# Probability tiles as places for weight pieces, and another order in the first three steps of an attention and soft mixture-of-experts kernel

## The chip, the cores and the metric

The kernel runs on 1 core of one Trainium2 chip, in one launch. The metric is device time in microseconds (us); lower is better. Engines: TensorE (PE, with its weight loads as PEld), VectorE (DVE), ScalarE (ACT), GpSimd (POOL) and SyncE (SP), which here issues all transfers but one. The trace's line numbers are those of the kernel before.

## The reference

First block-sparse attention over 4 batches, 8 heads, 768 positions of width 64. Each query sees the keys less than 16 positions away, and 24 summaries: for each block of 32 keys the elementwise maximum, and for the values the mean. Then a soft mixture of experts over the 3072 rows of width 512.

```python
k_sum = k.reshape(B, H, nb, block, D).max(axis=3)
v_sum = v.reshape(B, H, nb, block, D).mean(axis=3)
scores_l = where(|i - j| < 16, scale * q @ k.T, -1e9)
scores_s = scale * q @ k_sum.T + log(block)
a = softmax(concat(scores_l, scores_s));  x = a @ concat(v, v_sum)

logits = x @ phi                              # 3072 rows, 32 slots
slot_input = softmax(logits, axis=0).T @ x    # 8 experts, 4 slots each
slot_out[e] = relu(slot_input[e] @ w1[e]) @ w2[e]
out = softmax(logits, axis=1) @ slot_out
```

## The kernel before, in words

**Layout.** A head block is half a batch: four heads. There are 8 of them, each in 3 steps of 256 queries (two tiles of 128), so 24 steps. For each chunk of 64 queries, one product covers the chunk's own 64 keys and 64 further columns: edge keys (16 to either side) and the 24 block keys. Own keys, edges and block keys lie in one tile per head block, `kk`, of which there are two; edges and block keys stand there once for each of the six query tiles of a head block. `k_max` (L177) takes the block maxima on VectorE in six parts, `k_put` (L201) copies them into the place of each query tile, `k_edge` (L189) copies the edges. The sums of the values (`v_sum`, "V" in the plan) are products on TensorE, a ScalarE copy and VectorE additions; `put_v` (L343) copies them into each step's value tile on GpSimd.

**A step** (the loop at L526). For step i: scores on TensorE (L230); the scan (L249), in which VectorE adds the mask and takes the maximum, 8 tiles; the exponential on ScalarE, for half of the tiles after a subtraction on GpSimd (`soft_sub`, L265). Then step i-1's probabilities are transposed on TensorE (`trans`, L271) and copied by ScalarE (`evac`, L276), and step i-2's products with the values follow (`values`, L287), with their normalisation on VectorE (`norm`, L308). PLAN (L41) says in which step the parts that belong to the experts' routing ("X", "L", "T", "D") and the value sums ("V") are put, before or after the values. Each engine runs its instructions in the order in which this loop writes them; a wait holds what is queued behind it on that engine. Each step's scores reuse the same two banks, so the scores of step i+1 wait for the scan of step i.

**Transfers.** SyncE issues keys, queries, values and weights, in the order in which the code writes them, each after a wait for its place. A step's value tile is one of seven and is loaded anew seven steps later.

**Weights.** w1 and w2 make 64 pieces of 512 KB. `room` (L128) lists the places for them: 20 tiles of their own, and tiles of the attention that are done, each with the step from which it may be taken; NPRE is their count. Piece k goes to place k modulo NPRE (`load_piece`, L137). LOADS (L63) says how many are issued in each step, and `loads(...)` (L589, L596, L614, L626) those behind the loop. The first product (L661) takes 32 pieces and after each issues the next load; the second (L699) takes the other 32, interleaved by END with the products that make the output (L725). The output leaves in ten transfers of 512 KB and, for the last two blocks of rows, four of 256 KB.

**Start.** A few products on zeros (L502) run while the first keys arrive. Then the maxima, edges (GpSimd) and block keys (VectorE) of head block 0, then the steps.

Of the kernel before, what the change touches and what calls it, by code (L numbers as in the profile page):

```python
# [9 lines left out]
F32 = mybir.dt.float32  # L10
# [8 lines left out]
NB = S // 32  # L19
HB = 2 * B  # L20
TPS = 3
NSTEP = HB * TPS
NTT = 2 * TPS
# [15 lines left out]


PLAN = {  # L41
    0: "| V0",
    2: "| V1",
    5: "| V2",
    6: "X0 X1 |",
# [14 lines left out]
}  # L60


LOADS = [0, 0, 0, 0, 1, 1, 1, 1, 1, 1, 1, 1, 1, 1, 1, 1, 1, 1, 1, 3, 3, 3, 3, 5]  # L63

# [8 lines left out]
def attention_soft_moe(  # L75
# [12 lines left out]
    nc = tc.nc  # L88
    NQ = NT // 512

    const = ctx.enter_context(tc.tile_pool(name="const", bufs=1))
    att = ctx.enter_context(ExitStack())
    wk = att.enter_context(tc.tile_pool(name="wk", bufs=2, side="right"))
# [21 lines left out]
    qs = [qb[:, n] for n in range(NQR)]  # L115
    vs = [const.tile([128, 2, 2, 4, 65], F32, name=f"v{n}") for n in range(NV)]
    xs = [const.tile([128, 2, 512], F32, name=f"x{n}") for n in range(NX)]
    was = [const.tile([128, 1024], F32, name=f"wa{n}") for n in range(NWA)]


    pieces = [("w1", e, c) for e in range(NE) for c in range(4)] + [("w2", n) for n in range(32)]
    vflat = [v.rearrange("p c t h d -> p (c t h d)")[:, 0:1024] for v in vs]
    qall = qb.rearrange("p n t r k -> p (n t r k)")
    qflat = [qall[:, 1024 * n : 1024 * n + 1024] for n in range(3)]
    xflat = [x.rearrange("p t c -> p (t c)") for x in xs]
    kflat = [[k[:, 1024 * n : 1024 * n + 1024] for n in range(3)] for k in kk]

    room = [(t, 0) for t in was] + [(vflat[3], 19), (vflat[4], 20)] + [(t, 20) for t in kflat[0] + [qflat[0]]]  # L128
    room += [(vflat[5], 21), (xflat[2], 21), (vflat[6], 22), (vflat[0], 23)]
    room += [(t, 23) for t in kflat[1] + qflat[1:]] + [(vflat[1], 24), (vflat[2], 25)]  # L130
    room += [(t, 26) for t in xflat[3:]] + [(t, 27) for t in xflat[0:2]]
    NPRE = len(room)
    slots_ = [t for t, _ in room]
# [23 lines left out]
    def load_q(hb, part=slice(0, TPS)):  # L157
        if hb < HB:
            nc.sync.dma_start(out=qs[hb % NQR][:, part], in_=qx[hb, :, part])
# [11 lines left out]
    def eview(hb, c):  # L171
        e0 = (EA0, 0)[c]
        return kk[hb % 2][:, e0 : e0 + NEH].rearrange("p (r t k) -> p r t k", r=2, t=NTT)

    kst = {}

    def k_max(hb, part):  # L177
        if hb >= HB:
            return
        if hb not in kst:  # L180
            kst[hb] = wk.tile([128, 2, NB], F32, name="ks", bufs=2)
        pr, th = part // 3, part % 3
        nc.vector.reduce_max(  # L183
            out=kst[hb][:, pr, 8 * th : 8 * th + 8],
            in_=kview(hb)[:, pr, 16 + 256 * th : 272 + 256 * th].rearrange("p (b k) -> p b k", k=32),
            axis=AX,
        )

    def k_edge(hb, eng):  # L189
        if hb >= HB:  # L190
            return
        k = kview(hb)
        for c in range(2):
            e = eview(hb, c)[:, :, :, 32 * c : 32 * c + 32]
            for half in range(2):
                o = 64 * c + 80 * half
                src = k[:, :, o : o + 128 * (NTT - 1) + 16]
                src = bass.AP(src.tensor, src.offset, [src.ap[0], src.ap[1], [128, NTT], [1, 16]])
                eng.tensor_copy(out=e[:, :, :, 16 * half : 16 * half + 16], in_=src)  # L199

    def k_put(hb, eng):  # L201
        if hb >= HB:
            return
        for c in range(2):
            o = 0 if c else 32
            eng.tensor_copy(  # L206
                out=eview(hb, c)[:, :, :, o : o + NB], in_=kst[hb].unsqueeze(2).broadcast_to([128, 2, NTT, NB])
            )

    def keys(hb, r, c, pr, t):  # L210
# [29 lines left out]
    def soft_max(i, r):  # L240
        hb, tp = steps[i]
        s = ps_[i][r]
        m = wk.tile([128, 4], F32, name="m", bufs=4)
        p = wk.tile([128, 4, 128], F32, name="p", bufs=4)
        for u in range(4):
            t = 2 * tp + u // 2
            mk = 0 if t == 0 else 2 if t == NTT - 1 else 1

            nc.vector.tensor_tensor_reduce(  # L249
                out=p[:, u, :], in0=s[:, u, :], in1=maskv[:, mk, :], scale=-0.125, scalar=-NEG,  # L250
                op0=ALU.add, op1=ALU.min, accum_out=m[:, u : u + 1],
            )
        p_[i, r] = p, m
# [18 lines left out]
        ptr_[i, r] = pt  # L272

    def evac(i, r, eng=None):
        ptr = wk.tile([128, 4, 128], F32, name="ptr", bufs=4)
        (eng or nc.scalar.copy)(out=ptr, in_=ptr_[i, r])  # L276
        ptr_[i, r] = ptr

# [64 lines left out]
    def put_v(i, c, eng):  # L343
        n0 = 0 if c else 96
        src = vsst[0:NB, i // TPS % 2].rearrange("n h c -> n (h c)").unsqueeze(1)
        eng.tensor_copy(  # L346
            out=vs[i % NV][n0 : n0 + NB, c].rearrange("n t h c -> n t (h c)"), in_=src.broadcast_to([NB, 2, 260])
        )
# [136 lines left out]
    def flush(gs):  # L485
        for g in gs:
            while advance(g):
                pass
# [3 lines left out]
    def begin(names):  # L492
        gs = [pieces_of[n[0]](int(n[1:])) for n in names.split()]
        for g in gs:
            advance(g)
        return gs
# [7 lines left out]
    load_k(0, 1)  # L504
    load_q(0, slice(0, 1))
    nc.scalar.dma_start(out=cs, in_=cst)
    for i in range(TPS):
        load_v(i)
    load_q(0, slice(1, TPS))
    load_k(1, 0)  # L510
    load_k(1, 1)
    for hb in range(2):
# [5 lines left out]
    for part in range(6):  # L518
        k_max(0, part)
    k_edge(0, nc.gpsimd)  # L520
    k_put(0, nc.vector)
    nc.gpsimd.memset(W1ST, 0.0)


# [1 line left out]
    for i in range(NSTEP):  # L526
        a, b = i - 1, i - 2
        front, back = (PLAN.get(i, "|")).split("|")
        hb, tp = i // TPS, i % TPS
        now[0] = i  # L530
        scores(i)
        if i < TPS:
            load_q(1, slice(tp, tp + 1))
            for n in ((3, 4), (5,), (6,))[i]:
                load_v(n)
        load_q(hb + 2, slice(tp, tp + 1))
        if tp == 2:
            load_k(hb + 2, 0)
        if tp == 0 and hb > 0:
            load_k(hb + 1, 1)  # L540
        held = [g for g in held if advance(g)]
        soft_max(i, 0)
        soft_exp(i, 0)
        flush(held)
        if a >= 0:
            for c in range(2):
                put_v(a, c, nc.gpsimd)
        for n in range(LOADS[i]):
            if now[0] < 19:
                load_piece(True)  # L550
        if tp == 2:
            k_put(hb + 1, nc.gpsimd)
        soft_max(i, 1)
        if i < NSTEP - 1:
            soft_sub(i, 1)
        if tp == 1:
            k_edge(hb + 1, nc.gpsimd)
        if a >= 0:
            trans(a, 0)
            trans(a, 1)  # L560
            evac(a, 0)
            evac(a, 1, nc.vector.tensor_copy if i == NSTEP - 1 else None)
        flush(begin(front))
        soft_exp(i, 1)
        if b >= 0:
            values(b)
            norm(b)
        if tp < 2:
            for part in ((0, 1, 2), (3, 4, 5))[tp]:
                k_max(hb + 1, part)  # L570
        held = begin(back)
        if b >= 0:
            load_v(b + NV)
        for _ in range(LOADS[i]):
            if now[0] >= 19:
                load_piece()


    def loads(step, n):
        now[0] = step  # L580
        for _ in range(n):
            load_piece()
# [3 lines left out]
        put_v(j, c, nc.gpsimd)  # L586
    trans(j, 0)
    values(j - 1)
    loads(24, 4)  # L589
    evac(j, 0)  # L590
    trans(j, 1)
    evac(j, 1)
    gx = begin("X18 X19")
    norm(j - 1)
    values(j)
    loads(25, 1)  # L596
    flush(gx)
    tail.append(1)
    norm(j)
# [30 lines left out]
    fin = ctx.enter_context(tc.tile_pool(name="fin", bufs=2, side="right"))  # L630
# [8 lines left out]

    for q0, n in ((0, 4), (4, 2)):  # L640
        l = lt[:, q0 : q0 + n].rearrange("p q t -> p (q t)")
        ct = fin.tile([128, 512], F32, name="ct")[:, 0 : 128 * n]
        cv = ct.rearrange("p (b s) -> p b s", s=NE * 4)
        cm = fin.tile([128, 16], F32, name="cm")[:, 0 : 4 * n]
        cz = fin.tile([128, 16], F32, name="cz")[:, 0 : 4 * n]
        nc.vector.transpose(out=ct, in_=l)
        nc.vector.reduce_max(out=cm, in_=cv, axis=AX)
        nc.vector.tensor_tensor(out=cv, in0=cv, in1=cm.unsqueeze(2).broadcast_to([128, 4 * n, 32]), op=ALU.subtract)
        nc.scalar.activation(out=ct, in_=ct, func=AF.Exp)
        nc.vector.reduce_sum(out=cz, in_=cv, axis=AX)  # L650
        nc.vector.tensor_scalar_add(out=cz, in0=cz, scalar1=EPS)
        nc.vector.reciprocal(out=cz, in_=cz)
        nc.vector.tensor_tensor(out=cv, in0=cv, in1=cz.unsqueeze(2).broadcast_to([128, 4 * n, 32]), op=ALU.mult)
        nc.vector.transpose(out=l, in_=ct)

    hps = pf.tile([128, 512], F32, name="hps", tag="pf")[:, 0:256]
    for k in range(32):
        _, e, c = pieces[k]
        t = wt[k].rearrange("p (j f) -> p j f", j=4)
# [177 lines left out]
```

## Time and profile before

| | |
|---|---|
| median of 3 runs | 194.75 us (194.31 to 195.47) |
| the profiled execution | 194.69 us, of which span 192.9 us |
| TensorE busy | 168.3 us (87%) |
| VectorE, ScalarE, GpSimd busy | 121.0, 94.5, 72.1 us |
| moved by DMA | 66.36 MB, mean 344 GB/s |
| mean granted TensorE clock | 0.957 |

The span runs from the first to the last instruction. Busy times overlap, as the engines work side by side. A granted clock of 1.0 is TensorE's full speed, 0.5 half of it. A DMA share near 1 means that all 16 DMA engines have a packet under way nearly all the time.

### The profile page before, as it was taken

To read this page: it belongs to the slowest core of one execution; us is meant where nothing else is said; L and a number is where in the kernel's file an instruction comes from. 1 tells how busy PE (TensorE), PEld (TensorE's weight loads), DVE (VectorE), ACT (ScalarE), POOL (GpSimd) and SP (SyncE) were. 2 spreads that over 40 slices of the span, in tenths; PEclk is the share of its full clock that TensorE was granted. 3 is DMA by queue.
4 is the path that set the end of the run, shared out by engine and by line. 5 is a ranking of instruction groups with operands and counts; after the bars stand their busy time and mean duration, and the time that the engine had idled before them with its cause. 6 is when DMAs were issued, how large, how long until landed. Compare 5 with 4: busy or idle time off the path is not lost.

```text
span 192.9 us, 8003 instructions
## 1 busy us (share of the span) xinstructions
PE 168.3 (87%) x3201; PEld 131.2 (68%) x3201; DVE 121.0 (63%) x626; ACT 94.5 (49%) x244; POOL 72.1 (37%) x146
## 2 busy tenths in 40 slices
PE   6496999988999979899999899989689989998920
PEld 5394887976968956787797696876267755756700
DVE  1758589696879678749968986944568220153630
ACT  2026666597676677756578676954210000042420
POOL 3425946848545844822855744700020000000000
PEclk9979699999999999999999999999979999999985
DMA  5999989998799999878899999889899999999995
GB/s 191 417 403 403 374 261 304 350 375 314 252 360 374 296 343 332 277 279 274 314 337 362 370 364 368 325 279 394 349 354 314 414 414 402 405 411 410 386 408 201
DMA packets 20485, 66.36 MB, mean 344 GB/s; under 512 B 2272, under 2 KB 2272, under 8 KB 20448
## 3 DMA queue, kind: packets, MB, share of 16 engines
q1 hardware_dynamic: 20304, 65.48, 91.8%
q8 instruction: 25, 0.41, 0.8%
q10 hardware_dynamic: 144, 0.37, 0.5%
q14 instruction: 12, 0.10, 0.1%
HBM read 59.55 MB, written 6.29 MB: 341 GB/s over the span
## 4 chain that ended last, share of the span: by engine, by line
PE 57%; ACT 14%; DVE 11%; issue 3%; POOL 2%; DVEq 0%; ACTq 0%; POOLq 0%
PE hps L661 8%; PE pt L271 8%; PE s L230 8%; PE o L287 7%; PE so L699 7%; PE pp L323 5%; PE op L725 4%; ACT ptr L276 4%; ACT xt L360 4%; ACT p L259 4%; DVE p L249 3%; PE pp L413 3%; PE pp L357 2%; PE pp L370 2%; DVE x L308 2%
## 5 line engine op out<-in xcount | busy, mean ns | idle before, releaser
L259 ACT ACTIVATE p<-p,m 128x128 f32<-128x128 f32 x100 | 32.0, 391 | 27.9 <-DVE m L249 27.8
L249 DVE CUSTOM_DVE_ANT_0 p<-s,cs 128x128 f32<-128x128 f32 x192 | 42.6, 286 | 4.5 <-PE s L230 4.0
L265 POOL TENSOR_TENSOR p<-m,p 128x512 f32<-128x512 f32 x23 | 23.9, 1040 | 44.5 <-DVE m L249 40.6
L230 PE MATMUL s<-kk,q 64*64 64x128 f32 x768 | 29.1, 280 | 4.3 <-DVE kk L206 2.4
L346 POOL COPY v<-vsst 24x520 f32<-24x520 f32 x48 | 29.5, 614 | 4.4 <-issue 1.6
L230 PEld LDWEIGHTS s<-kk,q 64*64 64x64 f32 x768 | 23.5, 136 | 9.9 <-issue 4.5
L271 PE MATMUL pt<-ident,p 128*128 128x128 f32 x192 | 28.7, 285 | 1.1 <-ACT p L261 0.7
L287 PE MATMUL o<-v,ptr 120*64 120x65 f32 (+1 forms) x768 | 28.5, 229 | 0.9 <-DVE x L308 0.9
L287 PEld LDWEIGHTS o<-v,ptr 120*64 120x64 f32 (+1 forms) x768 | 25.2, 141 | 5.1 <-issue 4.6
L276 ACT COPY ptr<-pt 128x512 f32<-128x512 f32 x47 | 24.7, 572 | 1.7 <-PE pt L271 1.7
L271 PEld LDWEIGHTS pt<-ident,p 128*128 128x128 f32 x192 | 20.7, 142 | 7.1 <-issue 3.6
L183 DVE TENSOR_REDUCE ks<-kk 128x8 f32<-128x256 f32 x48 | 17.0, 409 | 4.5 <-DMA kk<-kx 4.4
L261 ACT ACTIVATE p<-p 128x512 f32<-128x512 f32 x23 | 14.7, 638 | 8.6 <-POOL p L265 8.5
L308 DVE TENSOR_TENSOR x<-o,z 128x256 f32<-128x256 f32 x48 | 18.1, 418 | 0.8
L249 DVE DVE_READ_ACCUMULATOR2_ANT m<- 128x1 f32 x192 | 15.9, 83 | 0.0
L323 PE MATMUL pp<-v,cs 64*64 64x128 f32 x384 | 13.8, 283 | 0.8 <-ACT xt L360 0.8
L736 ACT COPY kk<-op 128x256 f32<-128x256 f32 (+1 forms) x7 | 3.0, 468 | 22.8 <-PE op L725 22.8
L323 PEld LDWEIGHTS pp<-v,cs 64*64 64x64 f32 x384 | 11.8, 141 | 1.7 <-ACT xt L360 1.2
L305 DVE TENSOR_SCALAR z<-o 128x8 f32<-128x8 f32 x24 | 4.0, 165 | 12.5 <-PE o L287 12.1
L357 PE MATMUL pp<-ident,x 128*128 128x128 f32 x88 | 11.6, 273 | 0.1
L199 POOL COPY kk<-kk 128x192 f32<-128x192 f32 x32 | 9.7, 345 | 4.5 <-DMA kk<-kx 4.5
L360 ACT COPY xt<-pp 128x512 f32<-128x512 f32 x21 | 11.4, 593 | 0.0
(130 smaller groups left out, 200.4 us busy)
## 6 DMA issues: line engine op xcount, KB each, us to landing
wa<-w SPq DMA_DIRECT2D x40, 512.0 KB, 7.0
v<-vx SPq DMA_DIRECT2D x24, 520.0 KB, 5.8
kk<-kx SPq DMA_DIRECT2D x16, 400.0 KB, 5.3
q<-qx SPq DMA_DIRECT2D x22, 256.0 KB, 4.8
v<-w SPq DMA_DIRECT2D x9, 512.0 KB, 8.6
kk<-w SPq DMA_DIRECT2D x7, 512.0 KB, 6.4
x<-w SPq DMA_DIRECT2D x5, 512.0 KB, 5.5
out<-kk SPq DMA_DIRECT2D x5, 512.0 KB, 5.9
```

Source lines behind the costliest of these rows:

```text
L183: nc.vector.reduce_max(out=kst[hb][:, pr, 8 * th : 8 * th + 8], in_=kview(hb)[:, pr, 16 + 256 * th : 272 + 256 * th].rearrange("p (b k) -> ...
L230: nc.tensor.matmul(s[r][64 * c : 64 * c + 64, u, :].rearrange("p (a k) -> p a k", a=2), lhsT=qs[hb % NQR][64 * r : 64 * r + 64, tp, pr, o ...
L249: nc.vector.tensor_tensor_reduce(out=p[:, u, :], in0=s[:, u, :], in1=maskv[:, mk, :], scale=-0.125, scalar=-NEG, op0=ALU.add, op1=ALU.min, ...
L259: nc.scalar.activation(out=p[:, u, :], in_=p[:, u, :], func=AF.Exp, scale=-1.0, bias=m[:, u : u + 1])
L265: nc.gpsimd.tensor_tensor(out=p, in0=m.unsqueeze(2).broadcast_to([128, 4, 128]), in1=p, op=ALU.subtract)
L271: nc.tensor.transpose(pt[:, u, :], p[:, u, :], ident)
L276: (eng or nc.scalar.copy)(out=ptr, in_=ptr_[i, r])
L287: nc.tensor.matmul(o[64 * c : 64 * c + 64, r, u, :], lhsT=ptr[0:K, u, 64 * c : 64 * c + 64], rhs=v[0:K, c, tt, 2 * pr + r, :], start=True, ...
L308: nc.vector.tensor_tensor(out=x[:, r], in0=o[:, r, :, 0:64].rearrange("p (t q) d -> p t q d", t=2), in1=z[:, r].rearrange("p (t q) -> p t ...
L323: nc.tensor.matmul(pv[c][64 * g : 64 * g + 64, 0:128].rearrange("p (h d) -> p h d", h=2), lhsT=cs[64 * c : 64 * c + 64, o : o + 64], rhs=v ...
L346: eng.tensor_copy(out=vs[i % NV][n0 : n0 + NB, c].rearrange("n t h c -> n t (h c)"), in_=src.broadcast_to([NB, 2, 260]))
L360: (nc.vector.tensor_copy if on_dve else nc.scalar.copy)(out=xt.rearrange("p c t -> p (c t)"), in_=pv)
```

## The change

Three things are changed.

1. The tiles for probabilities and for their transposes, until now four buffers each of a pool that ends with the attention, become two tiles of double size each, `p0`, `p1` and `ptr0`, `ptr1`, one pair per odd or even step. The four, 512 KB each, join the list of places, so NPRE goes from 41 to 45. LOADS and the counts behind the loop are set anew. To make room, the slots' softmax has one buffer `ct` for its two rounds.
2. The queries of step 1 are loaded ahead of the first three value tiles; until now they came in one transfer with those of step 2, behind the values.
3. In steps 0 to 2, V0 (the value sums of head block 0) moves from the end of step 0 into step 1, behind GpSimd's subtraction; step 0's sums are copied to its value tile after that. The maxima, edges and block keys of head block 1 move to the end of step 1 (three maxima) and into step 2 (the rest, on GpSimd behind the subtraction). Block keys of head block 0 are copied by VectorE for two of the six query tiles and by GpSimd for four.

```diff
 PLAN = {
-    0: "| V0",
+    1: "V0 |",
...
-LOADS = [0, 0, 0, 0, 1, 1, 1, 1, 1, 1, 1, 1, 1, 1, 1, 1, 1, 1, 1, 3, 3, 3, 3, 5]
+LOADS = [0, 0, 0, 0, 1, 1, 1, 1, 1, 1, 1, 1, 1, 1, 1, 1, 1, 1, 1, 4, 4, 4, 2, 7]
...
+    pbs = [const.tile([128, 2, 4, 128], F32, name=f"p{n}") for n in range(2)]
+    tbs = [const.tile([128, 2, 4, 128], F32, name=f"ptr{n}") for n in range(2)]
...
-    room += [(t, 23) for t in kflat[1] + qflat[1:]] + [(vflat[1], 24), (vflat[2], 25)]
+    room += [(t, 23) for t in kflat[1] + qflat[1:] + pflat[0:1]] + [(vflat[1], 24), (tflat[0], 24)]
+    room += [(t, 25) for t in (vflat[2], pflat[1], tflat[1])]
...
-    def k_put(hb, eng):
+    def k_put(hb, eng, t0=0, n=NTT):
...
-        p = wk.tile([128, 4, 128], F32, name="p", bufs=4)
+        p = pbs[i % 2][:, r]
...
-        ptr = wk.tile([128, 4, 128], F32, name="ptr", bufs=4)
+        ptr = tbs[i % 2][:, r]
...
+    load_q(0, slice(1, 2))
     for i in range(TPS):
         load_v(i)
-    load_q(0, slice(1, TPS))
+    load_q(0, slice(2, TPS))
...
     k_edge(0, nc.gpsimd)
-    k_put(0, nc.vector)
+    k_put(0, nc.vector, 0, 2)
+    k_put(0, nc.gpsimd, 2, 4)
     nc.gpsimd.memset(W1ST, 0.0)
...
-        if a >= 0:
+        if a > 0:
             for c in range(2):
                 put_v(a, c, nc.gpsimd)
...
-        if tp == 2:
+        if tp == 2 and hb > 0:
             k_put(hb + 1, nc.gpsimd)
         soft_max(i, 1)
         if i < NSTEP - 1:
             soft_sub(i, 1)
-        if tp == 1:
+        if i == 1:
+            flush(begin(front))
+            front = ""
+            put_v(0, 0, nc.gpsimd)
+            put_v(0, 1, nc.gpsimd)
+        if i == 2:
+            for part in (3, 4, 5):
+                k_max(1, part)
+            k_put(1, nc.gpsimd)
+        if tp == 1 and hb > 0:
             k_edge(hb + 1, nc.gpsimd)
+        if i == 2:
+            k_edge(1, nc.gpsimd)
...
-        if tp < 2:
+        if i == 1:
+            for part in (0, 1, 2):
+                k_max(1, part)
+        if tp < 2 and hb > 0:
...
-    loads(24, 4)
+    loads(24, 2)
...
-    loads(25, 1)
+    loads(25, 3)
...
-        ct = fin.tile([128, 512], F32, name="ct")[:, 0 : 128 * n]
+        ct = fin.tile([128, 512], F32, name="ct", bufs=1)[:, 0 : 128 * n]
```

## Rows read from the trace of the kernel before

**Rows 1.** Stages: length, busy us (instructions) per engine, clock, DMA share, GB/s.

```profile
24.00:101.00 77.00, 72.57 (x1573) 60.35 (x1567) 61.30 (x371) 53.08 (x139) 44.50 (x92) 1.00 0.91 315
...
136.80:142.50 5.70, 4.08 (x44) 2.74 (x46) 3.77 (x13) 0.51 (x3) 1.05 (x1) 0.97 0.90 336
142.50:149.00 6.50, 6.50 (x97) 4.40 (x92) 5.06 (x10) 1.01 (x2) 0.01 (x1) 0.76 0.92 318
149.00:181.40 32.40, 30.87 (x602) 20.68 (x594) 9.43 (x25) 4.12 (x11) 0.00 (x0) 1.00 1.02 409
```

**Rows 2.** TensorE's waits, 142 to 185 us: total us, times, longest.

```profile
PE so L712 <- DVE sos L709: 0.7, 1, 0.7
...
```

**Rows 3.** SyncE in order of time, 180.5 us to the end: start, length.

```profile
181.38 0.33 SPq L745 DMA_DIRECT2D out<-v  x1
182.27 2.10 SPq L745 DMA_DIRECT2D out<-kk  x3
184.46 2.33 SPq L738 DMA_DIRECT2D out<-q  x2
186.89 1.61 SPq L743 DMA_DIRECT2D out<-q  x2
```

**Rows 4.** Line 745 (whole outputs), 181.3 to 182 us: issue to landing.

```profile
DMA to landing us min/median/max: 4.3/4.3/4.3
```

**Rows 5.** Line 147 (weight pieces), 121 to 125.2 us: issue to landing.

```profile
DMA to landing us min/median/max: 3.7/4.1/4.5
```

**Rows 6.** SyncE in order of time, 120 to 143 us.

```profile
129.49 0.96 SPq L147 DMA_DIRECT2D v<-w  x2
136.84 3.08 SPq L147 DMA_DIRECT2D x<-w  x4
```

**Rows 7.** GpSimd in order of time, 6.5 to 10 us.

```profile
6.77 1.21 POOL L199 COPY kk<-kk 128x192 f32<-128x192 f32 x4 [4.50 <-DMA kk<-kx]
7.93 1.06 POOL L522 MEMSET W1ST<- 128x1152 f32 x1
```

**Rows 8.** Line 206 (block keys): ns min/median/max, first and last start.

```profile
L206 DVE COPY kk<-ks x2: 291/837/1383, 7.8 to 9.1; 128x288 f32<-128x288 f32 x2
```

**Rows 9.** TensorE in order of time, 0 to 30 us.

```profile
9.25 2.02 PE L230 MATMUL s<-kk,q 64*64 64x128 f32 x29 [2.44 <-DVE kk L206]
...
13.15 1.35 PE L230 MATMUL s<-kk,q 64*64 64x128 f32 x31
...
17.83 1.09 PE L230 MATMUL s<-kk,q 64*64 64x128 f32 x28 [0.41 <-DVE m L249]
...
22.57 1.59 PE L323 MATMUL pp<-v,cs 64*64 64x128 f32 x48
23.99 1.04 PE L230 MATMUL s<-kk,q 64*64 64x128 f32 x32
24.97 1.09 PE L271 MATMUL pt<-ident,p 128*128 128x128 f32 x8
```

**Rows 10.** VectorE in order of time, step 0's scan: its first and last row.

```profile
11.48 0.29 DVE L249 CUSTOM_DVE_ANT_0 p<-s,cs 128x128 f32<-128x128 f32 x1 [2.12 <-PE s L230]
...
13.17 0.08 DVE L249 DVE_READ_ACCUMULATOR2_ANT m<- 128x1 f32 x1
```

**Rows 11.** GpSimd in order of time, 13 to 24 us.

```profile
21.33 0.79 POOL L206 COPY kk<-ks 128x288 f32<-128x288 f32 x2
22.10 1.03 POOL L265 TENSOR_TENSOR p<-m,p 128x512 f32<-128x512 f32 x1
```

**Rows 12.** Stretches of equal clock at the start, columns as in rows 1.

```profile
9.08:12.50 3.42, 3.25 (x58) 3.28 (x62) 1.30 (x11) 0.69 (x3) 0.00 (x0) 0.50 1.02 406
12.50:15.91 3.41, 3.24 (x70) 2.52 (x62) 2.39 (x14) 1.37 (x5) 1.04 (x1) 1.00 1.04 407
15.91:19.32 3.41, 1.92 (x36) 1.52 (x36) 3.19 (x24) 2.64 (x7) 2.71 (x5) 1.00 1.03 397
19.32:22.74 3.42, 3.40 (x42) 2.70 (x44) 1.40 (x15) 2.34 (x7) 3.30 (x8) 0.50 1.05 395
```

More of the change, by code (lines that the diff above doesn't have):

```diff
@@ L124, in attention_soft_moe @@
     qflat = [qall[:, 1024 * n : 1024 * n + 1024] for n in range(3)]
+    pflat, tflat = ([t.rearrange("p r u k -> p (r u k)") for t in ts] for ts in (pbs, tbs))
     xflat = [x.rearrange("p t c -> p (t c)") for x in xs]
@@ L206, in k_put @@
             eng.tensor_copy(
-                out=eview(hb, c)[:, :, :, o : o + NB], in_=kst[hb].unsqueeze(2).broadcast_to([128, 2, NTT, NB])
+                out=eview(hb, c)[:, :, t0 : t0 + n, o : o + NB],
+                in_=kst[hb].unsqueeze(2).broadcast_to([128, 2, n, NB]),
             )
```

## The prediction

> **What bounds the kernel now.** The stages come first [rows 1]: for each stretch, how long each engine worked, the granted clock, and what the DMA engines moved. In the attention loop (24 to 101 us) TensorE is busy 72.57 of 77 us: the loop goes at TensorE's pace, and what brings it forward brings forward all that follows. From 149 to 181.4 us the DMA engines move 409 GB/s at a share of 1.02; they are full. Between 136.8 and 149 us they move only 336 and 318 GB/s.
>
> Next, the end. TensorE's longest wait after 142 us is 0.7 us, for VectorE [rows 2]; none of its waits there is for a transfer, so each weight piece lies ready before its product. Still the run ends on transfers. SyncE sends one output of 512 KB at 181.38 us, three more from 182.27 us on, and four halves from 184.46 us on, the last two at 186.89 us and later [rows 3]. These eight hold 3.15 MB, which at 409 GB/s is 7.7 us. So the end is the time at which the first of the eight has its data, its way to landing, and then full DMA engines.
>
> Last, the beginning, where the order changes: what holds VectorE's copy [rows 7, 8], TensorE's work in order [rows 9], the scan of the scores [rows 10], GpSimd's work [rows 11] and the clock [rows 12].
>
> **The tail: four more places for weights.** The places go from 41 to 45, so 2.1 MB more (5.1 us at 409 GB/s) are sent before the first product instead of during it. The new counts in LOADS do nothing by themselves: after step 18 SyncE's queue holds weight transfers alone, in a fixed order, each waiting for its place. The first new place is free when step 22's probabilities are transposed, in step 23, earlier than places ahead of it; the others with the transposes and values of steps 22 and 23, at about the time of the places v1 and v2. SyncE sends v1 and v2 from 129.49 us on and then nothing until 136.84 us, when an x place is free [rows 6]. The four go into that gap, and nothing that is needed soon stands behind them.
>
> What room do they fill? From 136.8 to 142.5 us there is 5.7 x (1 - 336/409) = 1.0 us, and up to 149 us 6.5 x (1 - 318/409) = 1.4 us [rows 1]; together 2.4 us of the 5.1. The rest only pushes other pieces back. So the weights end up to 2.4 us earlier, but the run doesn't: the output of 181.38 us waits for its data. It took 4.3 us to land [rows 4]; of two weight pieces sent singly between 121 and 125 us the quicker took 3.7 us [rows 5]. With no weights ahead of it, the output gains these 0.6 us, and the seven behind it follow at the same rate. I take 0.6 us for the tail; the bounds are 0 and 2.4 us.
>
> **The first copy.** Today VectorE writes the block keys of head block 0 for all six tiles in two copies. The first took 1383 ns against 291 ns for the second [rows 8]. It was due when the maxima ended at 7.76 us and ended only when GpSimd's memset of W1ST did, at 7.93 + 1.06 = 8.99 us [rows 7]; GpSimd had gone from its edge copies into the memset without a pause. After the change VectorE copies two tiles and GpSimd four, and GpSimd does so before the memset. Its copies have 192 elements, as the edge copies have, four of which took 1.21 us; two are 0.6 us. If VectorE is again held until GpSimd pauses, it is held 0.6 us longer, and the first scores start at 9.25 + 0.6 = 9.85 us. The other end: it is held only until the running edge copy ends, near 8.0 us; then two copies of at most 0.29 us give scores from about 8.4 us on. I take 9.85, since the one row that shows this case shows the long hold.
>
> The Trainium skill (SBUF — State Buffer, "Who interferes with whom") says that a VectorE copy in a two-port mode and a GpSimd instruction lock one port pair against each other, and that whoever issues first has it for the whole instruction. The row agrees that one of them is blocked fully, but VectorE came before the memset and still went after it. By the Trainium skill it would have had the ports after the edge copy that was running; that result is rival 1.
>
> **Steps 0 to 2.** Step 0: scores at half clock take 2.23 us (9.25 to 11.48) [rows 9, 10, 12], so they end at 12.1. Eight scans take 1.77 us (11.48 to 13.25) [rows 10], to 13.85. Step 1's scores wait for them (before, they started at 13.15, 0.1 us ahead of the last) and start at 13.75; at full clock 1.35 us, to 15.1. V0 no longer stands between the two, where it filled TensorE's wait; it comes now, at V1's pace (22.57 to 23.99) 1.42 us, to 16.5; the transposes 1.09 us, to 17.6; step 2's scores 1.04 us, to 18.6 [rows 9]. Before, they ended at 18.92, after a wait for VectorE, which had put V0's sum and three maxima ahead of step 1's scan.
>
> Step 3's scores then wait for the keys of head block 1. Their maxima, copies and edges stood in steps 0 to 2 and were hidden; now the second three maxima, the copies and the edges come last in step 2, behind GpSimd's subtraction. After step 2's scores: the scan 1.77, the subtraction 1.03 (with the maxima beside it), the copies 0.79, the edges 1.21 [rows 10, 11], together 4.8 us, so 23.4 us. Before it was 23.99 [rows 9]: 0.6 us gained, and kept, as the loop goes at TensorE's pace. TensorE's own work in between (transposes, values, V1) hides under the 4.8 us: it took 5.1 us before (18.92 to 23.99), 3.4 of them at half clock [rows 12], which is 3.4 us at full clock.
>
> **At no cost.** The tiles for probabilities and their transposes alternate over two steps as before, so no new wait. Step 1's queries ahead of the values make these 256 KB later, 0.64 us at 409 GB/s; V0 now starts over 3 us later. Step 0's copies of sums into the values stand behind step 1's subtraction on GpSimd, but their reader is step 2's values. One buffer instead of two for the softmax over slots: VectorE does both rounds in order anyway, beside the first product; without that cover, well under 1 us.
>
> **Sum.** The profiled execution took 194.69 us (span 192.9, 1.8 around it; the median shown is 194.75). Minus 0.6 and 0.6: 193.5 us.
>
> **Rivals.** 1: VectorE is held for one instruction only. Scores start 1.45 us earlier than in my sum, and all of steps 0 to 3 with them: 192.0 us. For it: GpSimd's new copies wait for VectorE's maxima, which may open a pause. Against it: [rows 8].
>
> 2: The clock. TensorE now waits between the scores of steps 0 and 1, busy for some 2.25 us of 9.08 to 12.50, where it was 3.25 and full clock followed. The stretch from 15.91 with 1.92 us was followed by half clock [rows 12]; 2.25 lies between, nearer the second. If 12.5 to 15.9 is at half clock, step 1's scores take 2.02 us [rows 9], 0.7 us more: 194.2 us, no change.
>
> 3: The other side, slower. The half clock lasts from 12.5 to 19.3 us, since TensorE keeps waiting for the slowed chain of scores, scan, keys. Those 5.6 us from 13.75 on then do 2.8 us of work, step 3's scores start 2.8 us later, at 26.2 us: 196.3 us. It is slower from the point at which they start after 25.6 us (23.99 plus the tail's 0.6 and 1.0).
>
> 4: The new places give nothing, as the engines have no room that more requests could fill: the tail's 0.6 us fall away, 194.1 us.
>
> One thing more can fall either way. From 142.5 to 149 us the clock is 0.76 [rows 1], 1.6 us of full clock lost as the first product starts; a shift of half a microsecond can move that stretch off the product, which the low end allows for.
>
> **Chances.** My sum 0.36, rival 1 0.24, rival 2 0.20, rival 3 0.12, rival 4 0.08. A measurement tells 0.5% (1.0 us) from no change, so faster is under 193.8: rival 1 nearly whole, some 0.6 of my sum, little of the rest, 0.50. Slower is over 195.7: rival 3 and a little of rival 2, 0.15. The rest, 0.35, is no change. The range goes from 191.7 (my sum without the lost clock, below rival 1) to 195.5 us, where most of rival 3 is out.
>
> **What would show it.** VectorE's first copy ends with the memset near 9.6 us (rival 1: near 8.2). Scores of steps 0 and 1 start at 9.85 and 13.75, those of step 3 at 23.4 with GpSimd's edges as the last to come. The clock is 1.0 from 12.5 to 19.3 (rivals 2 and 3: 0.5). SyncE sends some six weight pieces from 129 us on in place of two, and 136.8 to 149 us shows about 400 GB/s (rival 4: no more than before). The output that was sent at 181.38 us lands in 3.7 us. If step 3's scores start no earlier than 24, or the end moves by another amount than they do plus 0.6 us, the prediction is wrong.

## The result

The changed kernel takes 191.93 us (median of 4 runs, 191.49 to 192.36) against 194.63 us for the kernel before beside it: a ratio of 0.9855, with a 95% interval of 0.9816 to 0.9893. It is faster, by 2.7 us, inside the range that was given (191.7 to 195.5) and 1.6 us below the forecast of 193.5; rival 1 had 192.0. The time lies only 0.2 us above the low end of that range. The profiled execution took 191.89 us, with a span of 189.9.

One thing has to be known for all that follows: executions of one kernel spread over some 4 us (the kernel before, over all sessions, from 191.6 us at a mean clock of 0.980 to 196.1 at 0.952), so medians are compared, and ratios and their intervals leave out executions more than 1.5% above the fastest of their kernel, which is why a ratio need not be the quotient of the medians beside it. Profiles are compared only where a stretch can be set beside its like.

**The first copies.** First line 211 (block keys; ns min/median/max, then first and last start) in the changed kernel, then TensorE in order of time:

```profile
L211 POOL COPY kk<-ks x4: 342/382/422, 7.7 to 20.8; 128x192 f32<-128x192 f32 x2, 128x288 f32<-128x288 f32 x2
L211 DVE COPY kk<-ks x2: 275/324/374, 7.6 to 7.8; 128x96 f32<-128x96 f32 x2
```

```profile
7.95 1.43 PE L236 MATMUL s<-kk,q 64*64 64x128 f32 x32 [1.75 <-DVE kk L211]
10.57 0.44 PE L236 MATMUL s<-kk,q 64*64 64x128 f32 x4 [1.19 <-DVE m L255]
11.31 1.75 PE L236 MATMUL s<-kk,q 64*64 64x128 f32 x26 [0.30 <-DVE m L255]
...
16.29 1.10 PE L236 MATMUL s<-kk,q 64*64 64x128 f32 x32
...
19.43 1.10 PE L329 MATMUL pp<-v,cs 64*64 64x128 f32 x32
21.52 0.67 PE L329 MATMUL pp<-v,cs 64*64 64x128 f32 x16 [0.99 <-DMA v<-vx]
22.01 1.65 PE L236 MATMUL s<-kk,q 64*64 64x128 f32 x32
```

GpSimd in order of time, as [rows 7]:

```profile
6.59 1.20 POOL L204 COPY kk<-kk 128x192 f32<-128x192 f32 x4 [4.32 <-DMA kk<-kx]
7.74 0.63 POOL L211 COPY kk<-ks 128x192 f32<-128x192 f32 x2
8.31 1.06 POOL L530 MEMSET W1ST<- 128x1152 f32 x1
```

VectorE's first copy is no longer held: 275 ns, where [rows 8] had 1383. GpSimd makes no pause for it that these rows show: its edge copies end at 7.79 us, its block keys follow from 7.74 us on, and the memset follows these. So step 0's scores start at 7.95 us, before at 9.25 [rows 9], and those of step 3 at 22.01 in place of 23.99. Ahead of the latter TensorE now waits 0.99 us for a landing: V1 lacks the last values of head block 1. Of these 2.0 us, 1.6 are left in the last step (23). TensorE at step 23's scores, before and after:

```profile
121.37 1.10 PE L230 MATMUL s<-kk,q 64*64 64x128 f32 x32
```

```profile
119.76 1.10 PE L236 MATMUL s<-kk,q 64*64 64x128 f32 x32
```

Not all of this is the order's: in the first 24 us the profile before has two stretches at half clock [rows 12], the profile after has one. The profile of 1b below, with the old order and one such stretch, has step 3's scores at 22.90 and step 23's at 120.38 us.

**The tail.** The stages that answer to [rows 1], shifted by these 1.6 us (columns as there):

```profile
135.20:140.90 5.70, 4.08 (x48) 2.70 (x50) 3.77 (x13) 0.51 (x3) 1.05 (x1) 1.00 1.02 413
140.90:147.40 6.50, 6.50 (x96) 4.44 (x92) 5.18 (x10) 0.80 (x2) 0.01 (x1) 0.74 1.03 407
147.40:179.80 32.40, 30.87 (x602) 20.68 (x594) 9.44 (x25) 4.33 (x11) 0.00 (x0) 1.00 0.99 394
```

The two stretches that had 336 and 318 GB/s now have 413 and 407, and the long one after them has slack (0.99 and 394 against 1.02 and 409): the weights are through before the outputs come. The first late output, its landing by line 768 (179.7 to 180.2 us), and SyncE in order of time, as [rows 3, 4]:

```profile
DMA to landing us min/median/max: 2.6/2.6/2.6
```

```profile
179.79 0.33 SPq L768 DMA_DIRECT2D out<-q  x1
...
186.07 0.58 SPq L766 DMA_DIRECT2D out<-kk  x1
```

It lands in 2.6 us in place of 4.3. TensorE's last output products, before and after:

```profile
180.26 4.04 PE L725 MATMUL op<-lt,sls 32*128 32x512 f32 x24
```

```profile
178.67 4.05 PE L748 MATMUL op<-lt,sls 32*128 32x512 f32 x24
```

From their start to the end of the span it was 12.6 us and is 11.3: 1.35 us from the places, and 1.6 us from what lies ahead of step 23, together the 3.0 us of the spans. Of the 1.7 us that the landing gained, 1.35 reached the end.

### The profile page after: what moved, and what is told of

Its sections match the earlier page's. It is cut to its first block, busy times and chain, and to the rows that moved or that the text cites. A ratio compares the mean times of both kernels' runs of the same rounds, so it can differ in the third digit from the quotient of the medians.

```text
span 189.9 us, 7974 instructions
## 1 busy us (share of the span) xinstructions
PE 166.9 (88%) x3201; PEld 130.0 (68%) x3201; DVE 119.6 (63%) x626; ACT 94.8 (50%) x244; POOL 72.5 (38%) x148
## 4 chain that ended last, share of the span: by engine, by line
PE 58%; DVE 13%; ACT 13%; DMA 4%; POOL 4%; issue 4%; DVEq 0%; SPq 0%; ACTq 0%; POOLq 0%
PE s L236 10%; PE hps L684 8%; PE so L722 7%; PE o L293 7%; PE pt L277 6%; PE pp L329 5%; PE op L748 4%; DVE p L255 4%; ACT p L265 4%; ACT xt L366 4%; ACT ptr L282 4%; DMA kk<-kx 3%; PE pp L419 3%; PE pp L376 2%; DVE x L314 2%
## 5 line engine op out<-in xcount | busy, mean ns | idle before, releaser
L236 PE MATMUL s<-kk,q 64*64 64x128 f32 x768 | 29.7, 279 | 4.2 <-DVE kk L211 1.8
L293 PE MATMUL o<-v,ptr 120*64 120x65 f32 (+1 forms) x768 | 27.8, 225 | 0.9 <-DVE x L314 0.9
L277 PE MATMUL pt<-ident,p 128*128 128x128 f32 x192 | 27.4, 281 | 0.5 <-ACT p L267 0.3
L293 PEld LDWEIGHTS o<-v,ptr 120*64 120x64 f32 (+1 forms) x768 | 24.4, 137 | 5.0 <-issue 4.5
L255 DVE DVE_READ_ACCUMULATOR2_ANT m<- 128x1 f32 x192 | 15.9, 83 | 0.0
L329 PE MATMUL pp<-v,cs 64*64 64x128 f32 x384 | 14.3, 286 | 1.8 <-DMA v<-vx 1.0
L684 PE MATMUL hps<-wa,W1ST 128*32 128x256 f32 x160 | 10.5, 430 | 0.5 <-DVE rz L473 0.5
L759 ACT COPY wa<-op 128x256 f32<-128x256 f32 x2 | 0.6, 375 | 20.7 <-PE op L748 20.7
```

The source lines that it names most:

```text
L236: nc.tensor.matmul(s[r][64 * c : 64 * c + 64, u, :].rearrange("p (a k) -> p a k", a=2), lhsT=qs[hb % NQR][64 * r : 64 * r + 64, tp, pr, o ...
L255: nc.vector.tensor_tensor_reduce(out=p[:, u, :], in0=s[:, u, :], in1=maskv[:, mk, :], scale=-0.125, scalar=-NEG, op0=ALU.add, op1=ALU.min, ...
L277: nc.tensor.transpose(pt[:, u, :], p[:, u, :], ident)
L293: nc.tensor.matmul(o[64 * c : 64 * c + 64, r, u, :], lhsT=ptr[0:K, u, 64 * c : 64 * c + 64], rhs=v[0:K, c, tt, 2 * pr + r, :], start=True, ...
L329: nc.tensor.matmul(pv[c][64 * g : 64 * g + 64, 0:128].rearrange("p (h d) -> p h d", h=2), lhsT=cs[64 * c : 64 * c + 64, o : o + 64], rhs=v ...
L684: nc.tensor.matmul(hps[32 * j : 32 * j + 32, :], lhsT=W1ST[:, c, 32 * e : 32 * e + 32], rhs=t[:, j, :], start=(k == 0), stop=(k == 31), ti ...
```

## The experiments

Ratios are to the kernel before in the same session; three sessions of four kernels each, every session on another chip.

| kernel | median us | before us | ratio, 95% interval |
|---|---|---|---|
| changed, first measurement | 191.93 | 194.63 | 0.9855, 0.9816 to 0.9893 |
| 1a: 41 places | 192.94 | 193.99 | 0.9949, 0.9918 to 0.9979 |
| 1b: places alone | 191.94 | 193.99 | 0.9909, 0.9871 to 0.9946 |
| 1c: split undone | 193.11 | 193.99 | 0.9935, 0.9900 to 0.9971 |
| 1d: memset ahead | 192.95 | 193.99 | 0.9938, 0.9900 to 0.9975 |
| 2a: changed again | 191.70 | 194.04 | 0.9878, 0.9833 to 0.9922 |
| 2b: V0 in step 0 | 191.84 | 194.04 | 0.9888, 0.9843 to 0.9933 |
| 2c: fill at the tail | 190.63 | 194.04 | 0.9795, 0.9753 to 0.9838 |
| 2d: fill at both ends | 191.56 | 194.04 | 0.9875, 0.9828 to 0.9921 |
| 3a: queries behind | 193.07 | 194.14 | 0.9977, 0.9933 to 1.0021 |
| 3b: fill, 41 places | 192.81 | 194.14 | 0.9937, 0.9891 to 0.9983 |
| 3c: fill again | 190.69 | 194.14 | 0.9869, 0.9801 to 0.9937 |
| 3d: fill, values and edges earlier | 189.79 | 194.14 | 0.9805, 0.9747 to 0.9863 |

**1a, 41 places.** The four places out of the list, LOADS and counts as before.

```diff
-    room += [(t, 23) for t in kflat[1] + qflat[1:] + pflat[0:1]] + [(vflat[1], 24), (tflat[0], 24)]
-    room += [(t, 25) for t in (vflat[2], pflat[1], tflat[1])]
+    room += [(t, 23) for t in kflat[1] + qflat[1:]] + [(vflat[1], 24), (vflat[2], 25)]
```

> The changed kernel with the four new places taken out again (41 places, the counts of before); the new order of the first steps stays. Theory A (start and tail add up): the start is worth 1.6 us at step 23 and the places 1.3 us, as the first late output waited 4.3 us for its landing before and 2.6 us after; so the time goes up by 1.3 us, to 193.2 us, with step 23's scores unmoved at 119.8 us. My prediction's size: the places are worth 0.6 us, 192.5 us. Rival (rival 4 of the prediction, the places give nothing and all comes from the start): 191.9 us.

Measured: 0.9949, so the order is worth 1.0 us (0.4 to 1.6) without the places, some 40% of the gain. Its profile has step 23's scores at 119.72 us, as with the places. TensorE's last products, then the span:

```profile
177.80 4.05 PE L747 MATMUL op<-lt,sls 32*128 32x512 f32 x24
```

```profile
core 0: 190.8 us, clock 0.978
```

13.0 us from the one to the other. Here the first weight product ran at full clock, and TensorE was 0.9 us earlier than in the changed kernel; the end came 0.9 us later all the same. The tail's term is one of DMA.

**1b, the places alone.** The kernel before with `p0`, `p1`, `ptr0`, `ptr1`, the list, LOADS and counts of the change.

> The kernel before with the four new places alone; the order of the first steps as before. Theory A: 194.6 - 1.3 = 193.3 us, and the steps' scores stand where they stood before (step 23 at 121.4 us). My prediction's size: 194.0 us. Rival (places and start only work together, since without the shift the outputs have no room): 194.6 us.

Measured: 0.9909, 1.8 us (1.0 to 2.5). With 1a's 1.0 us that is 2.8, as much as both together within the noise: the two add up, and the rival that they work only jointly falls. But the median is also that of the changed kernel (191.94 beside 191.93 and, in 2a, 191.70), and the intervals overlap; that the order adds something is shown by 1a. And step 23's scores start at 120.38 us, where theory A had them unmoved at 121.4. From the last output products (179.46 us) to the span's end (190.8) it is 11.3 us with the old order too.

**1c, the split undone.**

```diff
-    k_put(0, nc.vector, 0, 2)
-    k_put(0, nc.gpsimd, 2, 4)
+    k_put(0, nc.vector)
```

> The changed kernel with VectorE copying the block keys of head block 0 for all six tiles, as before; GpSimd goes from its edge copies into the memset. Theory A: VectorE's first copy is held until the memset ends, near 8.8 us, the scores of step 0 start near 9.0 in place of 7.95 us, and the end moves by 1.0 us, 192.9 us. Rival: step 3's scores wait for the values of head block 1 (V1 waited 1.0 us for a landing at 21.5 us) and not for the start of step 0, so the delay is swallowed before step 3: 191.9 us.

**1d, the memset ahead of GpSimd's block keys.**

```diff
-    k_put(0, nc.gpsimd, 2, 4)
     nc.gpsimd.memset(W1ST, 0.0)
+    k_put(0, nc.gpsimd, 2, 4)
```

> The changed kernel with GpSimd's memset of W1ST ahead of its four tiles of block keys instead of behind them. Theory H1 (VectorE's copy is held as long as GpSimd goes on without a pause; in the changed kernel the wait of GpSimd's copies for the maxima let it in): VectorE's copies of two tiles end near 9.0 us, scores of step 0 near 9.0, 192.9 us. Rival H2 (copies of 96 elements are not held at all, those of 288 are): they end near 8.0 us as in the changed kernel, scores of step 0 near 7.95, 191.9 us.

In both the hold is back. Line 211 in 1c, then in 1d:

```profile
L211 DVE COPY kk<-ks x2: 290/837/1384, 7.5 to 8.8; 128x288 f32<-128x288 f32 x2
```

```profile
L211 DVE COPY kk<-ks x2: 1136/1210/1284, 7.6 to 7.8; 128x96 f32<-128x96 f32 x2
```

So the copies of 96 elements are held just as those of 288; the hold goes with the memset directly behind GpSimd's edge copies. Step 0's scores start at 8.94 and 8.98 us. What that costs at the end is less clear. Both medians lie 1.0 to 1.4 us above the changed kernel's two (ratios 0.9935 and 0.9938 against 0.9855 and 0.9878), but in other sessions, and the intervals overlap that of 2a. And in the profile of 1d, which has full clock throughout the start, the last third of V1 begins where it did:

```profile
8.98 1.22 PE L236 MATMUL s<-kk,q 64*64 64x128 f32 x32 [1.60 <-DVE kk L211]
...
21.46 0.67 PE L329 MATMUL pp<-v,cs 64*64 64x128 f32 x16 [1.73 <-DMA v<-vx]
21.95 1.09 PE L236 MATMUL s<-kk,q 64*64 64x128 f32 x32
```

One microsecond of late start is swallowed there by the wait for the values. Whether the split is worth anything at the end stays open.

**2a, the changed kernel again.**

> The changed kernel as it is, for a measurement beside the others. Theory B (three terms): the tail is worth 1.35 us whatever the clock does, since from TensorE's last output product to the end of the span it took 8.6 and 8.9 us with 41 places and 7.2 to 7.3 us with 45; the order of the first steps is worth 0.65 us at equal clock (step 23's scores at 119.7 us against 120.4 us, each with one half-clock stretch in the first 24 us); what is left is the number of half-clock stretches, which differs between executions of one kernel. So 2.0 us, a ratio near 0.990. If the ratio is again 0.9855 or less, the order is worth more than 0.65 us.

0.9878, 2.4 us; the interval holds both 0.990 and 0.9855.

**2b, V0 back in step 0.**

```diff
-    1: "V0 |",
+    0: "| V0",
...
-            flush(begin(front))
-            front = ""
```

> The changed kernel with V0 back at the end of step 0 (between the scores of steps 0 and 1); all else as changed. Theory B: step 3's scores wait for the landing of the last values of head block 1 (21.5 us) and for GpSimd's edges, not for step 1, so they start near 22 us all the same and the time is that of the changed kernel within 0.3 us, less where V0 keeps TensorE at work and the clock up. Rival (V0's move is what brings the start forward, as it stood in VectorE's way before step 1's scan): step 3's scores start at 23 us or later, and the time goes up by 1 us.

0.9888 beside 0.9878: V0's move shows no gain, with intervals of 0.45% to either side. Step 3's scores start at 22.34 us, as the theory had it.

**3a, the queries behind the values.**

```diff
-    load_q(0, slice(1, 2))
...
-    load_q(0, slice(2, TPS))
+    load_q(0, slice(1, TPS))
```

> The changed kernel with the queries of steps 1 and 2 in one transfer behind the three values, as before. Theory B (step 3 waits for the landing of the last values of head block 1 near 21.5 us and for GpSimd's edges): step 1's scores start near 12.4 in place of 10.5 us, since these queries land near 12.4, step 3's still near 22 us, and the time is that of the changed kernel, ratio 0.988. Rival (the early queries are what bring the start forward): step 3's scores 1 us or more later, ratio 0.993.

The theory lost to the rival. TensorE's start:

```profile
12.53 2.10 PE L236 MATMUL s<-kk,q 64*64 64x128 f32 x32 [3.05 <-DMA q<-qx]
...
23.02 0.43 PE L236 MATMUL s<-kk,q 64*64 64x128 f32 x2 [0.93 <-POOL kk L204]
23.60 1.20 PE L236 MATMUL s<-kk,q 64*64 64x128 f32 x30 [0.15 <-POOL kk L204]
```

Step 1's scores wait 3.05 us for their queries, and two steps on the chain that the prediction drew (scan, subtraction, copies, edges) ends last and puts step 3's scores at 23.0 to 23.6. The ratio of 0.9977 is 1% above the changed kernel's, in another session, and the intervals don't overlap; the quotient of the medians, 0.9945, is 0.7 to 0.8% above. So asking for one 256 KB transfer earlier is worth about as much as the whole new order in 1a, and without it the other changes of the first steps show no gain over the places alone (1b, 0.9909).

**2c, fill at the tail.** Six products on constants in TensorE's waits between the last transposes and the first weight product; nobody reads their result. One of the four places:

```diff
+    def fill(n):
+        f = ps_s.tile([128, 4, 128], F32, name="s0")
+        for _ in range(n):
+            nc.tensor.matmul(f[:, 0, :], lhsT=ident, rhs=cs[:, 0:128], start=True, stop=True)
...
-    flush([slots()])
+    gs = slots()
+    advance(gs)
+    fill(2)
+    flush([gs])
```

> The changed kernel with six products on constants, whose result nobody reads, in TensorE's four waits between the last transposes and the first weight product. Theory B: where the half-clock stretch falls on the first weight product (15.7 us for it in four of six profiles, 14.0 us in the two without), TensorE loses 1.7 us; if the fill keeps the clock at full, the first weight product takes 14.0 us and the end comes 1.1 us earlier, no more, as the DMA engines stood idle for only 1.1 us before the last outputs. Rival: it is the narrow products themselves that lower the clock, and the fill changes nothing but adds up to 0.4 us.

0.9795 against 0.9878 beside it: 1.1 us less. The first 160 weight products (ns min/median/max) in the changed kernel, then here:

```profile
L684 PE MATMUL hps<-wa,W1ST x160: 376/379/634, 140.2 to 150.3; 128*32 128x256 f32 x160
```

```profile
L695 PE MATMUL hps<-wa,W1ST x160: 377/379/403, 141.0 to 149.4; 128*32 128x256 f32 x160
```

None runs at half clock any more: 8.4 us from the first to the last in place of 10.1. One profile would prove little, as three of the nine without a fill are free of it too (1a, 1c, 2b); but all five with it are (2c, 2d, 3b, 3c, 3d).

**2d, fill at both ends.** Three products more before the first keys and three behind step 0's scores.

> The same, and also three more products on zeros before the first keys and three behind step 0's scores, in TensorE's waits there. Theory B: no half-clock stretch in the first 24 us, step 23's scores at 119.0 us as in the one profile that had none, against 119.8 us: 0.7 us less than with the fill at the tail alone. Rival: the start is set by landings and by GpSimd up to step 3, the clock there costs nothing, and the time is that of the tail's fill alone.

0.9875, 0.9 us above 2c's median: no gain from the second fill. TensorE is at full clock up to V1 here, but so it is in 2c, which has no fill at the start; it then waits longer for the same landing. This kernel, and its clock after that:

```profile
21.58 0.67 PE L329 MATMUL pp<-v,cs 64*64 64x128 f32 x16 [1.97 <-DMA v<-vx]
```

```profile
22.60:25.90 3.30, 3.30 (x38) 2.64 (x32) 2.34 (x18) 2.04 (x7) 0.38 (x1) 0.50 0.97 376
```

What the start gains is lost to that wait and to half clock in step 3 (step 4's scores at 26.71 us, in the changed kernel at 25.70). 2c's profile has the same, so it does not explain the 0.9 us between the two. The spans of the two profiles lie 1.6 us apart: TensorE pauses for 0.86 us at 108.9 us here for no reason that the profile shows, and the first late output lands in 3.6 us in place of 2.9. Whether the other executions have either, no trace tells; the 0.9 us stay open.

**3b, the fill with 41 places.**

> The fill in TensorE's waits at the tail, with 41 places in place of 45. Theory B: with 41 places the DMA engines are full from 149 us to the end, so TensorE's 1.7 us from the clock give nothing and only the order of the first steps is left: ratio 0.995, as with 41 places and no fill; from TensorE's last product to the end of the span 8.6 us or more. Rival (TensorE sets the end in either case, the places only shorten the last stretch): the fill gives its 1.1 us here too, ratio 0.989.

0.9937, as 1a without fill (0.9949). TensorE is the earliest of the three profiles with 41 places, and the end is not (1a: 190.8 us). Last output products, then the span:

```profile
177.33 4.05 PE L758 MATMUL op<-lt,sls 32*128 32x512 f32 x24
```

```profile
core 0: 191.1 us, clock 0.981
```

13.7 us apart. With 41 places TensorE's gain at the tail shows nowhere in the time; with 45 it does (2c). There it has its limit too: with the fill the DMA engines are busy again just before the first late output (a share of 0.78, 0.84 and 0.87 in the 0.8 us ahead of it in 2c, 3c and 2d, in the changed kernel 0.09), and it lands in 2.9, 3.8 and 3.6 us in place of 2.6.

**3c and 3d, the values and the edges earlier.** Both with the tail's fill.

> The changed kernel with the tail's fill once more, as a measure for the next one on the same chip: ratio 0.980.

0.9869 (0.9801 to 0.9937), where 0.980 was expected: by its ratio the fill is no better here than the changed kernel. The medians say otherwise, 190.69 us beside 190.63 in 2c and 191.70 to 191.93 for the changed kernel. So some 1 us from the fill is likely, and its size isn't settled.

```diff
-            for n in ((3, 4), (5,), (6,))[i]:
+            for n in ((3, 4, 5), (), (6,))[i]:
...
             put_v(0, 1, nc.gpsimd)
+            k_edge(1, nc.gpsimd)
...
-        if i == 2:
-            k_edge(1, nc.gpsimd)
```

> The changed kernel with the tail's fill; the last values of head block 1 are asked for right behind the two before them (ahead of two transfers of queries), and GpSimd copies the edges of head block 1 in step 1 instead of step 2. Theory B: the values land 1.3 us earlier, near 20.2 us, and the edges are done before step 2's subtraction, so the scores of step 3 start near 21.3 in place of 22.0 to 22.4 us and the end moves with them: 0.7 us less than with the fill alone, ratio 0.976. Rival (from step 4 on the loop waits for VectorE, which swallows it): ratio 0.980.

```profile
19.80 0.67 PE L329 MATMUL pp<-v,cs 64*64 64x128 f32 x16 [0.62 <-DMA v<-vx]
20.44 1.56 PE L236 MATMUL s<-kk,q 64*64 64x128 f32 x32
```

The last third of V1 and step 3's scores come 1.6 to 1.7 us earlier than in the changed kernel, TensorE's wait for the values is down from 1.97 us (2c, 2d) to 0.62, and no half clock follows: step 4's scores start at 24.04 us. The median is 189.79 against 190.69 us beside it, 0.9 us less where 0.7 was expected, though the intervals overlap (0.9747 to 0.9863 and 0.9801 to 0.9937). It is the lowest median of all, 4.4 us under the kernel before; its interval still overlaps those of the changed kernel's two measurements (from 0.9816 and from 0.9833 on).

## Why the prediction was right or wrong

**What bounds: right.** The loop follows TensorE (in the two profiles 1.6 of 2.0 us at step 3 are still there at step 23), and the end follows the outputs' DMA behind the first late one (1a, 3b).

**The tail: right in mechanism, the term mis-sized.** Of "the output gains these 0.6 us" 1.35 was measured. The way to landing with nothing ahead was taken as 3.7 us, from a weight piece [rows 5]; the late output needed 2.6. That row didn't show what it was taken for: the DMA engines were at a share of 0.87 and 326 GB/s from 121 to 125.2 us, and at 0.09 in the 0.8 us ahead of the late output. The room was read right: the two stretches filled to 413 and 407 GB/s, and rival 4 falls.

**The first copy: wrong, and this is the step that failed.** The time came out inside the range, but not for this step's sake: "If VectorE is again held until GpSimd pauses", which put step 0's scores at 9.85 us (measured: 7.95), took GpSimd's own copies for something that holds VectorE as the memset did. They did not: 275 and 374 ns. 1d shows that the hold is real where the memset follows the edge copies at once. GpSimd's new copies differ from the memset in three ways: they wait for VectorE's maxima (done by 7.6 us, ahead of their turn), they read SBUF, and each takes 0.34 us in place of 1.06. No run tells which of them lets VectorE in. The rule of the Trainium skill (SBUF — State Buffer, "Who interferes with whom"), that, of a VectorE copy in a two-port mode and a GpSimd instruction, the first to issue has the ports for the whole of it, fits the changed kernel, and fits the second copy of 1d, which came after the memset had begun; it does not fit the first one there, issued at 7.60 us before the memset of 7.76 us and held all the same. No row shows in which mode these copies ran.

**Steps 0 to 2: the chain was right, its start and one wait were not.** Scan, subtraction, copies and edges do end last before step 3's scores when step 1 is late (3a). But "At no cost" missed the queries: once VectorE's copy isn't held, step 1's scores would wait for them until 12.5 us, so their move, priced at nothing, is worth about 1 us (0.7 to 1%, 3a). And the landing of head block 1's values, which the sum didn't have, sets the start of step 3 at 22 us. The chain is close behind: GpSimd's edges end at 22.4 us, and step 3's scores, 1.65 us long at full clock in place of 1.10, wait for them in part. V0's own move, on which the working for steps 0 to 2 spends much, measured nothing (2b).

**The clock.** The changed kernel in the stretches of [rows 12] (columns as there):

```profile
9.08:12.50 3.42, 1.94 (x38) 1.51 (x34) 1.78 (x16) 1.46 (x5) 1.33 (x2) 0.82 1.03 407
12.50:15.91 3.41, 3.41 (x66) 3.24 (x59) 1.94 (x17) 1.99 (x6) 1.04 (x1) 0.68 1.05 408
15.91:19.32 3.41, 3.41 (x77) 2.91 (x74) 3.26 (x22) 3.06 (x8) 2.45 (x4) 1.00 1.02 394
19.32:22.74 3.42, 2.35 (x65) 1.80 (x64) 2.14 (x8) 1.67 (x4) 3.19 (x8) 1.00 1.07 398
```

TensorE does wait there as rival 2 said, and half clock follows into V0; but there is time to spare before the values land, and step 3's scores don't feel it. The wait alone doesn't decide it: in 1d, 2c, 3b, 3c and 3d TensorE is busy for the same 1.94 us of 9.08 to 12.50 us, and full clock follows. Rival 3 did not come in this kernel: 15.9 to 22.7 us is at full clock. Step 23's scores lie at 119.0 to 119.8 us in six profiles with the new order whole or nearly so (the changed kernel twice, 1a, 1d, 2b, 3b), but at 120.6 to 121.6 in 2c, 3c and 2d, which have half clock in step 3, and at 121.2 in 1c, with two half-clock stretches in a row. The loss at the first weight product, which the low end allowed for, did not go away (0.74 from 140.9 to 147.4 us); by 2c it costs some 1.1 us. That low end is also not what the sum gives: 193.5 less 1.6 us is 191.9, not 191.7.

**The sum.** Forecast 0.6 + 0.6 = 1.2 us. Measured in the profiles 1.35 + 1.6 = 2.95 (span), in medians 2.3 to 2.7 us, about twice the forecast. Rival 1's time (192.0) came out, on its mechanism for the copy, but with its start cut short by the values' landing and its tail larger; that the two errors made up for each other is luck. By its own last sign the prediction fails: step 3's scores came 2.0 us earlier, and the end moved by 3.0, not by 2.0 + 0.6.

## What to carry to other kernels

Where the last stage runs on full DMA engines, look at whether earlier loads stand in the queue ahead of the first late output: as long as they did here, faster compute at the tail gave nothing (3b). When a step of the start is brought forward, list the landing of every operand of the next three steps; the next late one is the new bound, and a small transfer asked for earlier can be worth as much as all reordering on the engines (3a). Before a landing time is read off a row as that of an empty queue, look at the DMA share in that stretch. Where half clock falls on dense products behind a wait, a few idle products in that wait can pay (2c, some 1 us).

## What the runs showed of the hardware that was not expected

A VectorE copy issued 0.16 us before a GpSimd memset waited for the whole of that memset (1284 ns, 1d), and the same copy ahead of GpSimd copies took 275 ns. And a 512 KB output sent at a DMA share of 0.09 landed in 2.6 us; it took 2.6 us in seven of the eleven profiles with 45 places, 2.9 to 3.8 in the others (1c, 2c, 2d, 3c), and 4.3 to 5.4 with 41.
